# The order of a slot in a fused attention and mixture-of-experts kernel: first layer, second layer, then the attention's transposes, values and scores

## The chip, the cores and the metric

The kernel runs on one core of a Trainium2 chip. The metric is the time of one execution on the device in microseconds, the median of several runs. A core has the engines PE (matrix products, with its weight loads shown apart as PEld), DVE (vector), ACT (scalar functions), POOL (elementwise work of the GpSimd engine) and SP (here it only issues transfers). Each engine works its own instructions off in order and waits on semaphores for the others.

## What is computed

Sparse attention feeds a mixture of eight experts. Of the reference, cut:

```python
scores = scale * q @ k.T                       # 4 batches, 8 heads, 576 positions, 64 wide
scores = where(masks, scores, -1e9)            # heads 0-3: a local band of 32; heads 4-7: every 32nd position
attn = exp(scores - max); attn /= sum + 1e-9
x = (attn @ v) laid out as (2304, 512)
P = exp(x @ w_gate - max)                      # (2304, 8), then 8 rounds of row and column scaling
for e in range(8):
    out += P[:, e:e+1] * (relu(x @ w1[e]) @ w2[e])   # w1: 512 x 1024, w2: 1024 x 512
```

Products of the experts are made of three matmuls each, of operands split into a high and a low part (`split`: ACT writes the high part, POOL the difference).

## The kernel before

The attention is cut into 32 steps (`steps`, `NS`), each two heads by half a sequence. A step goes through these pieces: `at_scores` (PE, tile `sc`, line 251, in 64-row tiles of the array), `at_masks` (DVE, line 270, one instruction with its accumulator read per block), `at_exp` (ACT, line 281, one per block; a step has 4, 5 or 6 blocks), `at_normalize` (DVE lines 291 and 292, then a multiplication on POOL, line 293), `at_transpose` (PE, tile `tp`, line 303, then DVE copies to `pt`, lines 307 and 309), `at_values` (PE, tile `pv`, line 329, again in 64-row tiles), `x_high` (ACT, line 361) and `x_low` (DVE, line 366), which write the attention's output x into `reg`.

After a warm-up that runs the first eight steps, the rest of the attention is mixed with the first half of expert 0's hidden units in *slots*. Slot number s (0 to 35) does one 256-token chunk by one 128-wide piece `ft` of the hidden layer: `layer1` makes the product x·w1 (PE, tile `ph`, line 450, 12 matmuls) and `rectify` turns it into the hidden piece `h` (ACT, line 467: high part; DVE, line 468: low part); `layer2` multiplies the hidden piece of the slot before with w2 (PE, tile `y`, line 487, 6 matmuls; the last piece of a chunk is copied out by ACT, line 494 or 497, two copies). In slots 0 to 26 the attention rides along (`busy`): slot s takes the scores of step `at_k` = s + 8, the values of step `at_k - 3`, the transposes of step `at_k - 2` and the normalization of step `at_k - 1`. Where a chunk starts at a multiple of 512 tokens (slots 8, 16 and 24, `fresh`), its last block of x comes from the values of the same slot, so three quarters of the first layer (9 matmuls) stand at the slot's start and the last 3 behind the second layer.

The order in which the code of a slot is written is the order on every engine (`manual_schedule`): nothing is reordered later. Slots 0 to 3 also split the weights that are still missing (`late`: the last w1 piece in slot 0, the w2 pieces 1, 2, 3 in slots 1, 2, 3), at the slot's end, behind the step's exponentials on ACT and its multiplication on POOL; w2 piece `ft` is first read by the `layer2` of the next slot. In slots 5, 7, 9 to 12 and 18 to 23 a prepared sum of x blocks is split at the slot's end (`build_s`: ACT line 584, then DVE line 586). In slots 6, 13, 20 the gating's matmuls and in 7, 14, 21 its transposes are added (`next(gat)`).

PSUM is used in pairs of banks by tag: `l1` for `ph` and the gating, `y` and `s` for the second layer and the scores, `t` for the transposes and for the two value tiles of a step.

Of the kernel before, what the change touches and what calls it, by code (L numbers as in the profile page):

```python
# [8 lines left out]
F32 = mybir.dt.float32  # L9
# [57 lines left out]
def kernel(  # L67
# [10 lines left out]
    P = 128  # L78
# [14 lines left out]
    ps = ctx.enter_context(tc.tile_pool(name="ps", bufs=2, space=bass.MemoryType.PSUM))  # L93
# [62 lines left out]
    def store_x(n_parts):  # L156
        for _ in range(min(n_parts, len(done))):
            ci, k = done.pop(0)
            n = min(CH, NT - ci * CH)
            nc.sync.dma_start(  # L160
                xd[:, :, k, ci * CH : ci * CH + n], chunk(ci)[:, :, k].bitcast(F32)
            )
# [33 lines left out]
    def split_w(u, ft, which):  # L196
        src = raw.pop((u, ft, which))
        if which == 0:
            t = pools["w1"].tile([P, 2, NDT, P], F32R, tag="w1", name=f"w1_{u}_{ft}")
        else:  # L200
            t = w2t[:, 2 * D * ft : 2 * D * (ft + 1)].rearrange("p (b d) -> p b d", b=2)
        split(t[:, 0], t[:, 1], src)
        wt[u, ft, which] = t
# [9 lines left out]
    def load_qk(k):  # L213
        if k < NS:
            nq, nk, _ = _columns(*steps[k][1:])
            t = pools["qkv"].tile([P, QK], F32, tag="qk", name=f"qk_{k}", bufs=3)
            blocks = _blocks(*steps[k][1:])
            q0, ks, m = blocks[-1]
            end = nq + max(nk, ks[-1] + BR)
            nc.sync.dma_start(t[:, :end], qkv[k, :, :end])  # L220
            qk_t[k] = t
# [64 lines left out]
    def at_normalize(k):  # L286
        sm, n = sms[k]
        rs = sums_t.pop(k)[:, :n]
        if k in early:
            nc.vector.tensor_reduce(rs, sm[:, :n, :], axis=AX.X, op=ALU.add)  # L290
        nc.vector.tensor_scalar_add(rs, rs, 1e-9)
        nc.vector.reciprocal(rs, rs)
        nc.gpsimd.tensor_tensor(
            sm[:, :n, :], sm[:, :n, :], rs.unsqueeze(2).to_broadcast([P, n, BR]), op=ALU.mult
        )

    def at_transpose(k):
        sm, n = sms.pop(k)
        pt = pts[k] = pools["qkv"].tile([P, 3, P], F32, tag="pt", name=f"pt_{k}", bufs=3)
        tp = ps.tile([P, 3, P], F32, tag="t", name=f"tp_{k}")  # L300
        for c in range(0, n, 2):
            m = min(2, n - c)
            nc.tensor.transpose(  # L303
                tp[: m * BR, c // 2, :],
                sm[:, c : c + m, :].rearrange("p n k -> p (n k)"), ident,
            )
        nc.vector.tensor_copy(pt[:, : n // 2, :], tp[:, : n // 2, :])
        if n % 2:
            nc.vector.tensor_copy(pt[:BR, n // 2, :], tp[:BR, n // 2, :])
# [49 lines left out]
    def x_high(k):  # L359
        for src, (hi, _) in moved[k]:  # L360
            nc.scalar.activation(hi, src, AF.Copy)

    def x_low(k):
        b = steps[k][0]
        for src, (hi, lo) in moved.pop(k):
            nc.vector.tensor_tensor(lo, src, hi.bitcast(F32), op=ALU.subtract)
        p, hf = steps[k][1:]
        if hf:
            done.extend(
                (c, p) for c in range(NC) if b * S < min(NT, (c + 1) * CH) <= (b + 1) * S  # L370
            )
# [67 lines left out]
    def begin_layer1(u, c, ft, dts):  # L439
        c0, n = c  # L440
        k = u, c0, ft
        w = wt[u, ft, 0]
        first = k not in begun
        if first:
            begun[k] = ps.tile([P, 4 * P], F32, tag="l1", name=f"ph_{u}_{c0}_{ft}"), []
        ph, taken = begun[k]
        for dt in dts:
            taken.append(dt)
            for i, x in ((0, 0), (0, 1), (1, 0)):
                nc.tensor.matmul(  # L450
                    ph[:, :n], w[:, i, dt, :], xv(x, dt, c0, n),
                    start=(first and len(taken) == 1 and i + x == 0),
                    stop=(len(taken) == NDT and i == 1),
                )

    def layer1(u, c, ft, between=0):
        taken = begun[u, c[0], ft][1] if (u, c[0], ft) in begun else ()
        begin_layer1(u, c, ft, [dt for dt in range(NDT) if dt not in taken])
        for _ in range(between):
            next(gat)  # L460
        rectify(u, c, ft)

    def rectify(u, c, ft):
        c0, n = c
        ph = begun.pop((u, c0, ft))[0]
        h = pools["h"].tile([P, 2, 4 * P], F32R, tag="h", name=f"h_{u}_{c0}_{ft}")
        nc.scalar.activation(h[:, 0, :n], ph[:, :n], AF.Relu)
        nc.vector.scalar_tensor_tensor(
            h[:, 1, :n], ph[:, :n], 0.0, h[:, 0, :n].bitcast(F32), op0=ALU.max, op1=ALU.subtract
        )  # L470
        hs[u, c0, ft] = h
# [3 lines left out]
    def layer2(u, c, ft, only=None):  # L475
        c0, n = c
        nt = n // P
        if ft == 0 and (u, c0) not in ys:
            tags = ("y", "y", "s", "s")
            ys[u, c0] = [  # L480
                ps.tile([P, D], F32, tag=tags[i], name=f"y_{u}_{c0}_{i}") for i in range(nt)
            ]
        h, w = hs[u, c0, ft], wt[u, ft, 1]
        for i in range(nt) if only is None else only:
            y = ys[u, c0][i]
            for a, b, first in ((0, 0, True), (0, 1, False), (1, 0, False)):
                nc.tensor.matmul(  # L487
                    y, h[:, a, i * P : (i + 1) * P], w[:, b, :],
                    start=(ft == 0 and first), stop=(ft == FH - 1 and a == 1),
                )  # L490
            if ft == FH - 1:
                t = c0 // P + i
                if t < HEAD:
                    nc.scalar.activation(acc[:, t, :], y, AF.Copy)
                else:
                    o = acc[:, HEAD + t % STAGE, :]
                    nc.scalar.activation(o, y, AF.Copy)
                    outbox.append((yd[:, t - HEAD, :], o))
# [40 lines left out]
    for p in range(NPASS):  # L539
        for k in range(NK):  # L540
            k = (k - KEEP * p) % NK
# [527 lines left out]
    at_k = 0  # L1069

    def attention_scores():
        if at_k < NS:
            at_scores(at_k)
            at_masks(at_k)
            at_exp(at_k)

    def attention_rest():


        nonlocal at_k  # L1080
        if 0 <= at_k - 2 < NS:
            at_transpose(at_k - 2)
        if 0 <= at_k - 1 < NS:
            at_normalize(at_k - 1)
        at_k += 1

    def attention_values():
        if at_k > WARM + 2:
            store_x(1)
        if at_k > WARM + 1:  # L1090
            at_values(at_k - LAG, "tt")
            x_high(at_k - LAG)
            x_low(at_k - LAG)
        load_qk(at_k + 2)
        load_v(at_k)
# [66 lines left out]
    at_k = WARM + 1  # L1162
# [51 lines left out]
    slots = [(0, (c, 2 * P), ft) for c in range(0, NT, 2 * P) for ft in range(FH)]  # L1214
    prev, keep = None, []
    for slot, (u, c, ft) in enumerate(slots):
        busy = at_k < NS + LAG
        fresh = busy and ft == 0 and c[0] and c[0] % CH == 0
        if fresh:
            begin_layer1(u, c, ft, (0, 1, 2))  # L1220
        else:
            layer1(u, c, ft, ahead_of_second.get(slot, 0))
        if slot == 1:
            layer2(*prev, (0,))
        if busy:
            attention_values()
            attention_scores()
        if slot == 1:
            layer2(*prev, (1,))
        if slot == len(slots) - 1:  # L1230
            rest = [(prev, None), ((u, c, ft), None)]
        elif slot > 1:
            layer2(*prev)
        if fresh:
            begin_layer1(u, c, ft, (3,))
        if slot in (6, 7, 13, 14, 20, 21):
            next(gat)
        if slot < 2:
            load_w()
        if busy:  # L1240
            attention_rest()
            if fresh:
                rectify(u, c, ft)
            if slot in late:
                split_w(*plain[late[slot]])
            if slot == 5:
                split_gate()
            if at_k == NS + LAG:
                store_x(len(done))
                open_pools("right", ("hg", 8))  # L1250
        for x in work.get(slot, ()):
            x()
        send, keep = keep, []
        for x in send:
            nc.sync.dma_start(*x)
        keep, outbox[:] = outbox[:], []
        prev = (u, c, ft)
# [136 lines left out]
```

## Time and profile before

| | us |
|---|---|
| median of 3 runs (1534.41 to 1534.9) | 1534.9 |
| the profiled execution's own time | 1533.58 |
| its span on the engines | 1531.8 |
| PE busy | 1522.9 |
| DVE busy | 1302.4 |
| POOL busy | 1042.1 |
| ACT busy | 546.2 |

Shares of the whole span say little about the slots, which are its first tenth; the stretch is read by its own rows. In a row of the order of time, the first number is the start and the second how long the merged group lasted; matmuls overlap, so what a group of them costs PE is the distance from its first start to the start of the next group. What stands in brackets is the idle time of that engine just before, and what ended it.

### The profile page before, as it was taken

To read this page: it belongs to the slowest core of one execution; us is meant where nothing else is said; L and a number is where in the kernel's file an instruction comes from. 1 tells how busy PE (TensorE), PEld (TensorE's weight loads), DVE (VectorE), ACT (ScalarE), POOL (GpSimd) and SP (SyncE) were. 2 spreads that over 40 slices of the span, in tenths; PEclk is the share of its full clock that TensorE was granted. 3 is DMA by queue.
4 is the path that set the end of the run, shared out by engine and by line. 5 is a ranking of instruction groups with operands and counts; after the bars stand their busy time and mean duration, and the time that the engine had idled before them with its cause. 6 is when DMAs were issued, how large, how long until landed. Compare 5 with 4: busy or idle time off the path is not lost.

```text
span 1531.8 us, 27904 instructions
## 1 busy us (share of the span) xinstructions
PE 1522.9 (99%) x10099; PEld 1446.4 (94%) x10099; DVE 1302.4 (85%) x2611; ACT 546.2 (36%) x1340; POOL 1042.1 (68%) x1055
## 2 busy tenths in 40 slices
PE   8999999999999999999999999999999999999999
PEld 6888989898999999999999999999999999999998
DVE  6665899999999999768888888888688888888888
ACT  7675344343443434242332222322323232222221
POOL 4566155656556565078888888888687787777874
PEclk9999999999999999999999999999999999999999
DMA  9878888888898888886877867777576676666662
GB/s 279 254 236 274 313 315 315 338 315 337 309 337 316 321 318 314 320 312 259 313 259 283 308 239 292 298 255 277 211 306 262 261 286 240 264 266 238 276 247 90
DMA packets 145625, 431.11 MB, mean 281 GB/s; under 512 B 35696, under 2 KB 89168, under 8 KB 130512
## 3 DMA queue, kind: packets, MB, share of 16 engines
q1 hardware_dynamic: 145200, 429.14, 75.3%
q8 instruction: 80, 1.31, 0.3%
q14 instruction: 57, 0.47, 0.1%
q10 hardware_dynamic: 288, 0.20, 0.0%
HBM read 284.54 MB, written 144.75 MB: 280 GB/s over the span
## 4 chain that ended last, share of the span: by engine, by line
PE 98%; DVE 1%; ACT 0%; DMA 0%; issue 0%; POOL 0%; SPq 0%; ACTq 0%; POOLq 0%; DVEq 0%
PE p L882 27%; PE bb L731 18%; PE yg L763 18%; PE bc L731 12%; PE ba L731 12%; PE y L487 3%; PE ph L450 3%; PE pv L329 1%; PE sc L251 1%; PE pl L378 1%; PE tp L303 1%; PE tr L912 0%; PE unread L1119 0%; DMA qk<-in_qkv 0%; ACT sm L281 0%
## 5 line engine op out<-in xcount | busy, mean ns | idle before, releaser
L890 DVE TENSOR_TENSOR total<-p,total 128x384 f32<-128x384 f32 x770 | 401.0, 557 | 0.8 <-PE p L882 0.8
L731 PE MATMUL bb<-reg 128*128 128x384 f32 x1620 | 326.3, 336 | 0.0
L731 PEld LDWEIGHTS bb<-reg 128*128 128x128 f32 x1620 | 285.2, 188 | 2.9 <-DVE u L805 0.3
L731 PE MATMUL bc<-reg 128*128 128x384 f32 x1080 | 216.3, 334 | 0.0
L731 PE MATMUL ba<-reg 128*128 128x384 f32 x1080 | 216.2, 334 | 0.0
L863 ACT ACTIVATE a<-u 128x384 fp32r<-128x384 f32 x114 | 59.9, 526 | 384.5 <-DVE u L857 382.7
L805 DVE TENSOR_TENSOR u<-bb,m 128x384 f32<-128x384 f32 x180 | 99.8, 554 | 110.9 <-PE bb L731 109.5
L731 PEld LDWEIGHTS bc<-reg 128*128 128x128 f32 x1080 | 190.1, 188 | 0.0
L731 PEld LDWEIGHTS ba<-reg 128*128 128x128 f32 x1080 | 190.0, 188 | 0.0
L939 POOL TENSOR_TENSOR s1t<-m,u 128x384 f32<-128x384 f32 x57 | 57.9, 1016 | 163.3 <-DVE m L857 163.3
L770 DVE SCALAR_TENSOR_TENSOR acc<-yg,gate,acc 128x512 f32<-128x512 f32 x197 | 139.1, 740 | 9.0 <-PE yg L763 9.0
L763 PE MATMUL yg<-w2t,h 128*128 128x512 f32 x540 | 125.5, 390 | 0.0
L763 PE MATMUL yg<-w2b,h 128*128 128x512 f32 x540 | 125.4, 390 | 0.0
L882 PE MATMUL p<-s,w2b 128*128 128x384 f32 x696 | 125.3, 334 | 0.0
L882 PEld LDWEIGHTS p<-s,w2b 128*128 128x128 f32 x696 | 121.1, 188 | 0.0
L882 PE MATMUL p<-s,w2t 128*128 128x384 f32 x672 | 121.0, 334 | 0.0
L763 PEld LDWEIGHTS yg<-w2t,h 128*128 128x128 f32 x540 | 101.1, 188 | 20.5
L763 PEld LDWEIGHTS yg<-w2b,h 128*128 128x128 f32 x540 | 101.1, 188 | 20.5
L867 POOL TENSOR_TENSOR a<-u,a 128x384 fp32r<-128x384 f32 x114 | 117.0, 1026 | 0.0
L882 PEld LDWEIGHTS p<-s,w2t 128*128 128x128 f32 x672 | 116.9, 188 | 0.0
L194 POOL TENSOR_TENSOR reg<-ra,reg 128x512 fp32r<-128x512 f32 x28 | 48.1, 1719 | 89.3 <-ACT reg L193 89.3
L805 DVE TENSOR_TENSOR u<-bc,u 128x384 f32<-128x384 f32 x180 | 99.4, 552 | 4.5 <-PE bc L731 1.4
(154 smaller groups left out, 2810.2 us busy)
## 6 DMA issues: line engine op xcount, KB each, us to landing
reg<-wd SPq DMA_DIRECT2D x56, 1792.0 KB
wd<-reg SPq DMA_DIRECT2D x30, 1792.0 KB
w2b<-w2d SPq DMA_DIRECT2D x27, 1792.0 KB
w2t<-w2d SPq DMA_DIRECT2D x26, 1792.0 KB
w2d<-w2b SPq DMA_DIRECT2D x15, 2048.0 KB
w2d<-w2t SPq DMA_DIRECT2D x15, 2048.0 KB
raws<-in_w SPq DMA_DIRECT2D x68, 256.0 KB
reg<-sd SPq DMA_DIRECT2D x12, 768.0 KB
```

Of the source, the lines that this page charges most:

```text
L194: nc.gpsimd.tensor_tensor(lo, src, hi.bitcast(F32), op=ALU.subtract)
L450: nc.tensor.matmul(ph[:, :n], w[:, i, dt, :], xv(x, dt, c0, n), start=(first and len(taken) == 1 and i + x == 0), stop=(len(taken) == NDT ...
L487: nc.tensor.matmul(y, h[:, a, i * P : (i + 1) * P], w[:, b, :], start=(ft == 0 and first), stop=(ft == FH - 1 and a == 1),)
L731: nc.tensor.matmul(out[:, :TN], w[:, i, k, :], xops[x][:, xi, k, :], start=(start and n == 0), stop=(n == 5), skip_group_check=True,)
L763: nc.tensor.matmul(y, hg[g, i // 3, f][:, a, o : o + P], w[:, b, f, :], start=(f == 0 and a + b == 0), stop=(f == 1 and a == 1),)
L770: nc.vector.scalar_tensor_tensor(acc[:, i, :], y, gate[:, t, e : e + 1], acc[:, i, :], op0=ALU.mult, op1=ALU.add)
L805: nc.vector.tensor_tensor(o, bank[:, :TN], s, op=ALU.add)
L863: nc.scalar.activation(t[:, 0], src, AF.Copy)
L867: nc.gpsimd.tensor_tensor(t[:, 1], src, t[:, 0].bitcast(F32), op=ALU.subtract)
L882: nc.tensor.matmul(y[:, :TN], w[:, b, wi, d, :], h[:, a, :], start=(a + b == 0), stop=(a == 1),)
L890: nc.vector.tensor_tensor(o, y[:, :TN], o, op=ALU.add)
L939: nc.gpsimd.tensor_tensor(s1, m1, u3, op=ALU.add)
```

## The change

In a slot, the second layer moves ahead of the attention. Behind it the attention's transposes and the normalization come first, then values and scores; they were the slot's end before. In a fresh slot the transposes also move to the front of the attention, and the second layer stays behind it. Slots 0 and 1 keep their order. From slot 2 on, the transposes' tile is taken from the pair of banks `l1` in place of `t`.

```diff
--- before.py
+++ after.py
@@ -294,10 +294,10 @@
             sm[:, :n, :], sm[:, :n, :], rs.unsqueeze(2).to_broadcast([P, n, BR]), op=ALU.mult
         )
 
-    def at_transpose(k):
+    def at_transpose(k, tag="t"):
         sm, n = sms.pop(k)
         pt = pts[k] = pools["qkv"].tile([P, 3, P], F32, tag="pt", name=f"pt_{k}", bufs=3)
-        tp = ps.tile([P, 3, P], F32, tag="t", name=f"tp_{k}")
+        tp = ps.tile([P, 3, P], F32, tag=tag, name=f"tp_{k}")
         for c in range(0, n, 2):
             m = min(2, n - c)
             nc.tensor.transpose(
@@ -1074,15 +1074,11 @@
             at_masks(at_k)
             at_exp(at_k)
 
-    def attention_rest():
-
-
-        nonlocal at_k
+    def attention_turn(tag="t"):
         if 0 <= at_k - 2 < NS:
-            at_transpose(at_k - 2)
+            at_transpose(at_k - 2, tag)
         if 0 <= at_k - 1 < NS:
             at_normalize(at_k - 1)
-        at_k += 1
 
     def attention_values():
         if at_k > WARM + 2:
@@ -1220,17 +1216,23 @@
             begin_layer1(u, c, ft, (0, 1, 2))
         else:
             layer1(u, c, ft, ahead_of_second.get(slot, 0))
+        if slot == len(slots) - 1:
+            rest = [(prev, None), ((u, c, ft), None)]
+        elif slot > 1 and not fresh:
+            layer2(*prev)
         if slot == 1:
             layer2(*prev, (0,))
         if busy:
+            if slot > 1:
+                attention_turn("l1")
             attention_values()
             attention_scores()
-        if slot == 1:
-            layer2(*prev, (1,))
-        if slot == len(slots) - 1:
-            rest = [(prev, None), ((u, c, ft), None)]
-        elif slot > 1:
-            layer2(*prev)
+            if fresh:
+                layer2(*prev)
+            if slot == 1:
+                layer2(*prev, (1,))
+            if slot < 2:
+                attention_turn()
         if fresh:
             begin_layer1(u, c, ft, (3,))
         if slot in (6, 7, 13, 14, 20, 21):
@@ -1238,7 +1240,7 @@
         if slot < 2:
             load_w()
         if busy:
-            attention_rest()
+            at_k += 1
             if fresh:
                 rectify(u, c, ft)
             if slot in late:
```

The first of three places is PE in slots 2 and 3. `ph_0_0_2` is slot 2's first layer, `y_0_0_0` and `y_0_0_1` are the two token tiles of the second layer, `tp_8` the transposes of step 8, `pv_7` the values of step 7, `sc_10` the scores of step 10. Before:

```order
L450 MATMUL ph_0_0_2_796<-reg_107,w1_0_2_582 128x256 x12
L329 MATMUL pv_7_0_813<-pt_7_784,v_7_585 64x32 x2
...
L251 MATMUL sc_10_0_846<-qk_10_658 64x64 x2
...
L487 MATMUL y_0_0_0_713<-w2t_106,h_0_0_1_710 128x512 x3
L487 MATMUL y_0_0_1_714<-w2t_106,h_0_0_1_710 128x512 x3
L303 MATMUL tp_8_882<-cst_97,sm_8_682 128x128 x2
L450 MATMUL ph_0_0_3_891<-reg_107,w1_0_3_704 128x256 x12
```

With the change:

```order
L450 MATMUL ph_0_0_2_796<-reg_107,w1_0_2_582 128x256 x12
L487 MATMUL y_0_0_0_713<-w2t_106,h_0_0_1_710 128x512 x3
L487 MATMUL y_0_0_1_714<-w2t_106,h_0_0_1_710 128x512 x3
L303 MATMUL tp_8_819<-cst_97,sm_8_682 128x128 x2
L329 MATMUL pv_7_0_827<-pt_7_783,v_7_585 64x32 x2
...
L251 MATMUL sc_10_0_860<-qk_10_658 64x64 x2
...
L450 MATMUL ph_0_0_3_891<-reg_107,w1_0_3_704 128x256 x12
```

The second layer, and with it the first reader of the w2 piece split in the slot before, follows the first layer at once; values and scores stand behind it.

The second place is DVE in slots 9 and 10, from the low part of slot 9's sum (`so`) to the masks of step 18. `pt_15` and `pt_16` are copies of transposes, `sums_16` and `sums_17` row sums for the normalization, `reg_107<-pv_15` is x's low part. Before:

```order
L307 COPY pt_15_1571<-tp_15_1572 128x256
L309 COPY pt_15_1571<-tp_15_1572 64x128
L291 TENSOR_SCALAR sums_16_1442<-sums_16_1442 128x4
L292 RECIPROCAL sums_16_1442<-sums_16_1442 128x4
L586 TENSOR_TENSOR so_0_0_128_1581<-sx_0_0_128_1479,so_0_0_128_1581 128x512
L468 SCALAR_TENSOR_TENSOR h_0_512_2_1604<-ph_0_512_2_1591,h_0_512_2_1604 128x256
L366 TENSOR_TENSOR reg_107<-pv_15_0_1608,reg_107 128x192
L366 TENSOR_TENSOR reg_107<-pv_15_1_1609,reg_107 128x128
L270 ISA sm_18_1654,mx_18_1655<-sc_18_0_1639,cst_97 128x64
```

With the change:

```order
L586 TENSOR_TENSOR so_0_0_128_1581<-sx_0_0_128_1479,so_0_0_128_1581 128x512
L468 SCALAR_TENSOR_TENSOR h_0_512_2_1604<-ph_0_512_2_1591,h_0_512_2_1604 128x256
L307 COPY pt_16_1613<-tp_16_1614 128x256
L291 TENSOR_SCALAR sums_17_1570<-sums_17_1570 128x4
L292 RECIPROCAL sums_17_1570<-sums_17_1570 128x4
L366 TENSOR_TENSOR reg_107<-pv_15_0_1622,reg_107 128x192
L366 TENSOR_TENSOR reg_107<-pv_15_1_1623,reg_107 128x128
L270 ISA sm_18_1668,mx_18_1669<-sc_18_0_1653,cst_97 128x64
```

The copies and the two operations on the row sums stood between the masks and the sum's low part; now they stand between the hidden piece's low part and x's.

The third place is PE in the fresh slot 8. Before:

```order
L450 MATMUL ph_0_512_0_1389<-reg_107,w1_0_0_417 128x256 x9
L329 MATMUL pv_13_0_1399<-pt_13_1376,v_13_1114 64x54 x2
...
L487 MATMUL y_0_256_1_1143<-w2t_106,h_0_256_3_1298 128x512 x3
L450 MATMUL ph_0_512_0_1389<-reg_107,w1_0_0_417 128x256 x3
L303 MATMUL tp_14_1465<-cst_97,sm_14_1239 128x128 x2
L303 MATMUL tp_14_1465<-cst_97,sm_14_1239 64x128
L450 MATMUL ph_0_512_1_1486<-reg_107,w1_0_1_499 128x256 x12
L329 MATMUL pv_14_0_1503<-pt_14_1464,v_14_1213 64x32 x2
```

With the change:

```order
L450 MATMUL ph_0_512_0_1389<-reg_107,w1_0_0_417 128x256 x9
L303 MATMUL tp_14_1400<-cst_97,sm_14_1254 128x128 x2
L303 MATMUL tp_14_1400<-cst_97,sm_14_1254 64x128
L329 MATMUL pv_13_0_1409<-pt_13_1307,v_13_1132 64x54 x2
...
L487 MATMUL y_0_256_1_1090<-w2t_106,h_0_256_3_1298 128x512 x3
L450 MATMUL ph_0_512_0_1389<-reg_107,w1_0_0_417 128x256 x3
L450 MATMUL ph_0_512_1_1486<-reg_107,w1_0_1_499 128x256 x12
L487 MATMUL y_0_512_0_1502<-w2t_106,h_0_512_0_1474 128x512 x3
```

The last three matmuls of slot 8's first layer still wait for x from the values of this slot, whose low part DVE now writes behind the copies and the normalization; slot 9's second layer, which reads slot 8's hidden piece, follows slot 9's first layer at once.

## Rows read from the trace of the kernel before

**Rows 1.** The page: its span, and the chain that ended last, by engine.

```profile
span 1531.8 us, 27904 instructions
...
PE 98%; DVE 1%; ACT 0%; DMA 0%; issue 0%; POOL 0%; SPq 0%; ACTq 0%; POOLq 0%; DVEq 0%
```

**Rows 2.** Busy time by stretch: PE, PEld, DVE, ACT, POOL, granted clock, DMA share, GB/s.

```profile
10.00:20.00 10.00, 7.78 (x262) 6.43 (x251) 8.74 (x69) 8.85 (x44) 5.39 (x7) 1.00 0.91 279
```

**Rows 3.** PE in order of time, slots 9 to 11 (start, length, group).

```profile
63.51 1.67 PE L450 MATMUL ph<-reg,w 128*128 128x256 f32 x12
65.11 0.89 PE L329 MATMUL pv<-pt,v 64*64 64x32 f32 x40
...
66.31 1.66 PE L487 MATMUL y<-w2t,h 128*128 128x512 f32 x6
67.81 0.49 PE L303 MATMUL tp<-cst,sm 128*128 128x128 f32 x3
68.05 1.67 PE L450 MATMUL ph<-reg,w 128*128 128x256 f32 x12
...
72.47 0.72 PE L450 MATMUL ph<-reg,w 128*128 128x256 f32 x4
```

**Rows 4.** PE in order of time, a slot without attention.

```profile
155.26 1.68 PE L450 MATMUL ph<-reg,w 128*128 128x256 f32 x12
156.77 1.55 PE L487 MATMUL y<-w2t,h 128*128 128x512 f32 x6
```

**Rows 5.** All engines in order of time, slots 2 to 5.

```profile
32.59 2.07 PE L487 MATMUL y<-w2t,h 128*128 128x512 f32 x6
...
33.23 0.99 PEld L487 LDWEIGHTS y<-w2t,h 128*128 128x128 f32 x5 [0.46 <-POOL w2t L194]
...
34.63 1.68 PE L450 MATMUL ph<-reg,w 128*128 128x256 f32 x12
...
36.23 0.67 PE L329 MATMUL pv<-pt,v 64*64 64x32 f32 x32
...
37.21 1.92 PE L487 MATMUL y<-w2t,h 128*128 128x512 f32 x6
...
37.69 0.99 PEld L487 LDWEIGHTS y<-w2t,h 128*128 128x128 f32 x5 [0.29 <-POOL w2t L194]
...
39.10 1.67 PE L450 MATMUL ph<-reg,w 128*128 128x256 f32 x12
...
40.28 0.83 POOL L293 TENSOR_TENSOR sm<-sm,sums 128x384 f32<-128x384 f32 x1 [2.64 <-DVE sums L292]
...
42.40 1.01 PEld L487 LDWEIGHTS y<-w2t,h 128*128 128x128 f32 x5 [0.54 <-POOL w2t L194]
...
43.92 0.84 PE L450 MATMUL ph<-reg,w 128*128 128x256 f32 x5
```

**Rows 6.** DVE and ACT in order of time, from the masks of slot 9 to those of slot 10.

```profile
66.88 0.21 DVE L270 CUSTOM_DVE_ANT_0 sm<-sc,cst 128x64 f32<-128x64 f32 x1
...
67.14 0.35 ACT L281 ACTIVATE sm<-sm,mx 128x64 f32<-128x64 f32 x1 [0.60 <-DVE mx L270]
...
68.33 0.42 DVE L307 COPY pt<-tp 128x256 f32<-128x256 f32 x1 [0.79 <-PE tp L303]
...
68.94 0.63 ACT L584 ACTIVATE so<-sx 128x512 fp32r<-128x512 f32 x1 [0.36 <-POOL sx L581]
...
69.60 0.97 DVE L586 TENSOR_TENSOR so<-sx,so 128x512 fp32r<-128x512 f32 x1 [0.36 <-ACT so L584]
...
70.49 0.41 DVE L468 SCALAR_TENSOR_TENSOR h<-ph,h 128x256 fp32r<-128x256 f32 x1
...
70.95 0.55 DVE L366 TENSOR_TENSOR reg<-pv,reg 128x192 fp32r<-128x192 f32 x2
...
71.42 0.21 DVE L270 CUSTOM_DVE_ANT_0 sm<-sc,cst 128x64 f32<-128x64 f32 x1
```

**Rows 7.** ACT in order of time, slot 8: the two copies of a finished chunk.

```profile
63.67 1.06 ACT L494 ACTIVATE acc<-y 128x512 f32<-128x512 f32 x2
```

## The prediction

> **What bounds the kernel now.** I read the page first: PE carries 98% of the chain that ended last [rows 1], so anything that makes PE wait is paid in full, and what falls on another engine costs only where PE comes to wait for it. The time by stretch tells that the granted clock was 1.00 even where PE was busy for 7.78 us of 10 [rows 2]. Then the slots, in order of time on PE: in slot 9 the distances from group to group are 1.60 us for the first layer, 1.20 for values and scores, 1.50 for the second layer, 0.24 for the transposes, 4.54 in all [rows 3]; nothing is left between the groups that looks like a wait. The exceptions are slots 2, 3 and 4: there the second matmul of the second layer waits for POOL's low part of the w2 piece (L194 on w2t), and starts at 33.23, 37.69 and 42.40 [rows 5]. Last, DVE and ACT in a slot with a sum to split [rows 6], because the change reorders them too.
>
> The profiled execution took 1533.58 us by its own time, with a span of 1531.8; the median of the runs is 1534.9, 1.3 above it. I make the sum against 1533.6 and add 1.3. The measurement of this kernel can tell about 0.2%, 3.1 us, from no change.
>
> **What the change removes and adds.** No instruction, byte or transfer is added or dropped; 24 slots are reordered, and the loads and stores that SP issues keep their order among themselves. Four parts count.
>
> *The edges between full-array and 64-row matmuls.* Before, a slot goes from first layer to values and from scores to second layer; now from transposes to values and from scores to first layer: one entry and one exit either way. An entry costs 0.09: a first layer ahead of values takes 1.60 [rows 3], ahead of a second layer 1.51 [rows 4]. I take 0 for the difference, and 0.09 per slot either way as bounds, 24 x 0.09 = 2.2 us.
>
> *Slots 2 to 4, the w2 piece.* The split of a w2 piece stands behind the exponentials of the slot before, on ACT and then POOL, and its reader now comes ahead of values and scores, which so far ran while PE had to wait anyway. In slot 2 the wait ends as before at 33.23, since nothing ahead of it moved. Before, slot 3 began 1.40 later (34.63). Now values and scores, 1.20 by [rows 3], follow, with 0.15 for the entry (the 0.09 and a little for the transposes' last columns): slot 3 begins at 36.0, 1.4 late. From there it is a ring: scores, masks, exponentials, split on ACT, split on POOL, second layer, values, scores. Before, the reader's second matmul started 5.10 after the end of the scores in slot 3 (32.59 to 37.69) and 5.19 in slot 4 (37.21 to 42.40) [rows 5]. So slot 3's starts at 36.0 + 5.1 = 41.1, and slot 4 begins 1.41 + 0.98 + 0.15 later (old distance to the next first layer; values and scores, 36.23 to 37.21; entry), at 43.6 instead of 39.10. In slot 4 POOL's multiplication, 0.83 long, ran just ahead of the split's low part [rows 5]; it is now issued earlier, so I take 5.2 - 0.8: second matmul at 48.0, slot 5 at 48.0 + 1.52 + 0.98 + 0.15 = 50.7 instead of 43.92. That is **6.8 us**; 7.6 without POOL's 0.8, and 5.5 if each ring is another 0.6 shorter.
>
> *The fresh slots 8, 16, 24.* The last 3 matmuls of the first layer need x's low part, and DVE now writes it behind the copies of the transposes and the normalization, which in turn stand behind the sum's low part of the slot before. Pieces from [rows 3, 6]: masks begin 0.57 after the scores' end (66.31 to 66.88), the first exponential 0.26 later, 0.36 per block (four of them end at 68.94 - 0.36 = 68.58), the sum's high part 0.63, a hand-over of 0.03, its low part 0.89 until DVE goes on, copies and normalization 0.91 (68.33 to 69.60 - 0.36), x's low part 0.47. For slot 8, five blocks: 0.57 + 0.26 + 1.80 + 0.63 + 0.03 + 0.89 + 0.91 + 0.47 = 5.6 after slot 7's scores. PE is there after 9 of 12 matmuls (1.2), transposes 0.24, values and scores 1.20, second layer 1.50: 4.1. Wait 1.4. Next, the hidden piece of slot 8: masks at 5.6, then 0.26, four exponentials 1.44, the two copies of a finished chunk 1.06 [rows 7], about 0.4 for the ReLU: 8.7; its reader, slot 9's second layer, was 1.2 us of values and scores later and now comes at 5.6 + 0.4 + 1.6 = 7.6. Wait 1.1. Slot 16 follows a slot without a sum, so 1.55 falls away: no first wait, the second is 7.2 - 6.1 = 1.0. Slot 24 has no scores of its own: PE is there after 3.7, the first wait is 1.9, and the second goes. Together **5.4 us**; bounds 2 (half of it hidden, since these chains sum worst cases) and 8.
>
> *The slots with a sum to split, 5, 7, 9 to 12, 18 to 23.* Here DVE and ACT form a ring of one slot: masks, exponentials, sum high, sum low, hidden piece low, x low, next masks. Before, without the 0.36 that ACT waited for POOL, it is 0.26 + 1.44 + 0.63 + 0.03 + 0.89 + 0.46 + 0.47 = 4.2 with four blocks and 4.5 with five [rows 6], about PE's slot of 4.54: covered. The copies and the normalization lay beside the exponentials; now they lie in the ring, 0.91 more: 5.4. A slot of PE gains a lag of 0.9 on each. PE starts to pay when the hidden piece's low part comes later than the next first layer that needs its bank: it ended at 70.90 [rows 6] and that began at 72.47 [rows 3], so 1.57 is cover. Slots 9 to 12: 4 x 0.9 - 1.57 = 2.0. Of 18 to 23, two hold the gating's matmuls and are longer on PE; four count, another 2.0. Slots 5 and 7 stand alone and are covered. Together **4.0 us**; bounds 0 (the lag stays covered) and 7. In slots without a sum the ring is 4.4 with five blocks: covered. Taking `tp` from the first pair of banks costs nothing that I find: the bank it takes was last read by a slot's hidden piece or by the copies of the transposes, a slot earlier; what it was to give, fewer waits of the values for the `t` pair, the steady slots do not show as a wait.
>
> Sum: 0 + 6.8 + 5.4 + 4.0 = 16.2; 1533.6 + 16.2 + 1.3 = **1551 us**.
>
> **Rivals.** *First, the ring of w2 alone.* If DVE and ACT keep enough lead, the last two parts vanish: 1533.6 + 6.8 + 1.3 = 1541.7. For it speaks that steady slots show no wait now; against it the ring of 5.4 against 4.54. *Second, the edges decide, and it is not slower.* If grouping transposes, values and scores let both edges go, that would give back 0.09 at the entry and I allow as much at the exit: 24 x 0.18 = 4.3, and with the last two parts covered 6.8 - 4.3 leaves +2.5, 1537.4, within what cannot be told. It would decide from 0.16 per slot on; the number of edges speaks against it. *Third, the clock.* PE now waits for about 3 us in slots 3 and 4. If the granted clock fell to 1.2 GHz there and a slot of 4.5 us ran at that level after each, up to 2 x 4.5 = 9 more: 1560. Against it: the clock stayed at 1.00 with 2.2 us of 10 not busy [rows 2]. The Trainium skill, page "TensorE: Matmul & The Clock Gate", section "Part 1: The HAM clock gate (the "warmup" mystery)", states that a half-rate clock is the default and activity releases it, which speaks for this rival: by that rule, if these waits count as idle, the time would be the 1560; the trace shows no fall so far. That the change does not do what it says can be left out: the order of the instructions shows it.
>
> **How the numbers follow.** Forecast 0.78, first rival 0.10, second 0.04, third 0.05, and 0.03 for what I don't see, 0.02 of it faster and 0.01 no change. The low bounds of the parts give 5.5 + 2 + 0 - 2.2 = 5.3 (1540), the high ones 7.6 + 8 + 7 + 2.2 = 25 (1560); that all lie at one end is unlikely, so 1545 to 1557 is the forecast's own range, and 1541 to 1558 takes in the first rival and leaves the third out. Slower by over 0.2%: 0.78 + 0.10 + 0.05 = 0.93; within: 0.05; faster: 0.02.
>
> **What would show it.** In the profile after: the distance from slot 2's first layer to slot 5's grows by about 7 us, with PE or its weight loads waiting for POOL's L194 on w2t, about three times 1 to 3 us; behind each fresh slot's first layer waits for DVE's x (L366), and then of the second layer for ACT's or DVE's hidden piece (L467, L468); in slots 10 to 13 and 19 to 22 some tenths each before the first layer. Past slot 27 nothing changes but the start. I am wrong if slots 2 to 4 together grow by under 4 us, if slots 9 to 13 show no wait, or if the slots without waits differ from 4.54 and 4.42 by more than 0.1.

## The result, and the profile after

The changed kernel takes 1549.51 us (median of 5 runs, 1549.28 to 1551.84) against 1534.9 (5 runs, 1533.98 to 1535.49): 14.6 us more, a ratio of 1.0099 with a 95% interval of 1.0085 to 1.0113. The profiled execution took 1549.28 with a span of 1547.5. The page of the changed kernel, span and the chain that ended last by engine, answers to [rows 1]:

```profile
span 1547.5 us, 27910 instructions
...
PE 94%; ACT 3%; DVE 2%; issue 0%; POOL 0%; DMA 0%; ACTq 0%
```

PE had 98% of that chain; 4% of 1547 us, some 60 us, now run through ACT and DVE in its place. A chain runs through them for the whole time that they take, not only for the part that PE waits. What PE lost is read from the slots: the distance from the start of a slot's first layer (L450 on ph) to the start of the next one's, after less before. Of slot 0's first layer the warm-up makes the first nine matmuls; its start is that of the last three. This table has the distances in us for groups of slots, for the changed kernel and for the twelve of the experiments (E1 to E12); "others" are the rest of slots 0 to 26. From slot 28 on no distance in slots differs by more than 0.02.

| kernel | median us (runs) | ratio to before | 2 to 4 | 8, 9 | 16, 17 | 24, 25 | 6, 13, 20 | 7, 14, 21 | others | sum |
|---|---|---|---|---|---|---|---|---|---|---|
| the change | 1549.5 (5) | 1.0099 | 7.59 | 2.05 | 1.54 | 1.85 | 1.72 | -0.73 | 1.35 | 15.36 |
| E1 pair t | 1573.8 (5) | 1.0259 | 9.62 | 4.51 | 1.89 | 4.52 | 4.83 | 1.48 | 10.56 | 37.40 |
| E2 old in 2 to 4 | 1543.1 (5) | 1.0054 | 0.00 | 2.05 | 1.56 | 1.86 | 1.91 | -0.74 | 1.36 | 8.00 |
| E3 only transposes | 1539.8 (5) | 1.0038 | 0.13 | 1.42 | 0.91 | 1.71 | 1.19 | -0.14 | 0.12 | 5.35 |
| E4 early splits | 1542.5 (5) | 1.0051 | 0.02 | 2.05 | 1.54 | 1.86 | 1.70 | -0.72 | 1.40 | 7.85 |
| E5 sum ahead | 1542.5 (5) | 1.0060 | 7.30 | 0.58 | 1.61 | 0.29 | 0.36 | -0.72 | -0.13 | 9.29 |
| E6 old in 8, 9, ... | 1545.9 (5) | 1.0081 | 7.79 | 0.33 | 0.62 | 1.40 | 1.88 | -0.74 | 1.85 | 13.13 |
| E7 before, early splits | 1532.7 (11) | 0.9993 | -1.19 | 0.03 | -0.02 | 0.00 | 0.01 | 0.01 | -0.01 | -1.17 |
| E8 = E4 + E5 | 1535.5 (11) | 1.0012 | 0.00 | 0.58 | 1.64 | 0.29 | 0.36 | -0.72 | -0.13 | 2.02 |
| E9 = E8, w1 elsewhere | 1536.1 (1) | | 0.02 | 0.58 | 0.74 | 0.28 | 0.36 | -0.72 | 0.47 | 1.73 |
| E10 = E8, h first | 1535.2 (1) | | 0.02 | 0.14 | 1.17 | 0.29 | 0.36 | -0.73 | -0.15 | 1.10 |
| E11 = E8, copies late | 1537.6 (1) | | 0.03 | 1.42 | 2.47 | 0.29 | 0.36 | -0.72 | -0.14 | 3.70 |
| E12 one early split | 1546.1 (1) | | 5.23 | 2.05 | 1.53 | 1.86 | 1.73 | -0.74 | 1.35 | 13.00 |

Where two kernels do the same thing, their entries agree to some hundredths (2.05 in four of them), which the medians cannot offer: those are comparable to about 0.2%. The sum leaves out the warm-up ahead of slot 0, which no edit touches, and what stands behind the slots. Slot 0 started between 0.36 us earlier (E1) and 2.29 later (E2) than before, 0.65 later in the changed kernel, whose granted clock was 0.91 over the first 20 us; from slot 28 to the end the executions differ from the one before by -0.80 (E8) to 0.25 (E9).

Slots 2 to 5 on PE in order of time in the changed kernel, against [rows 5]:

```profile
30.45 1.68 PE L450 MATMUL ph<-reg,w 128*128 128x256 f32 x12
32.53 0.50 PE L487 MATMUL y<-w2t,h 128*128 128x512 f32 x1 [0.41 <-ACT w2t L193]
33.88 1.43 PE L487 MATMUL y<-w2t,h 128*128 128x512 f32 x5 [0.85 <-POOL w2t L194]
...
36.65 1.68 PE L450 MATMUL ph<-reg,w 128*128 128x256 f32 x12
40.22 0.50 PE L487 MATMUL y<-w2t,h 128*128 128x512 f32 x1 [1.89 <-ACT w2t L193]
41.57 1.71 PE L487 MATMUL y<-w2t,h 128*128 128x512 f32 x5 [0.85 <-POOL w2t L194]
...
45.34 1.95 PE L450 MATMUL ph<-reg,w 128*128 128x256 f32 x12
48.16 0.50 PE L487 MATMUL y<-w2t,h 128*128 128x512 f32 x1 [0.87 <-ACT w2t L193]
49.51 1.42 PE L487 MATMUL y<-w2t,h 128*128 128x512 f32 x5 [0.85 <-POOL w2t L194]
...
52.16 1.70 PE L450 MATMUL ph<-reg,w 128*128 128x256 f32 x12
```

The second layer now waits for both parts of its w2 piece, high (ACT) and low (POOL), in each of the three slots. From the second wait's end to the next first layer it takes 2.77 in slot 2 (33.88 to 36.65), 2.65 in slot 4 (49.51 to 52.16), and 3.77 in slot 3 (41.57 to 45.34). The stretches of the changed kernel tell why (columns as in [rows 2], the granted clock third from the end):

```profile
36.00:42.00 6.00, 3.27 (x56) 2.64 (x50) 2.15 (x18) 3.45 (x17) 1.88 (x2) 1.00 0.52 174
42.00:46.00 4.00, 4.00 (x62) 3.16 (x61) 1.62 (x12) 0.62 (x3) 0.83 (x1) 0.57 0.02 4
46.00:48.00 2.00, 1.29 (x11) 1.09 (x10) 0.37 (x6) 2.00 (x11) 0.00 (x0) 1.00 0.58 175
```

PE was busy for 3.27 of 6 us; behind that the granted clock fell to the 1.2 GHz level for most of 42 to 46, and was back by 46. It cost about 1.06 us, 3.77 less 2.71, the mean of its neighbours.

The other waits of PE in the changed kernel, as totals from 53 us to 170 us (what waits, for what, us in total, times, longest):

```profile
PE y L487 <- ACT h L467: 2.0, 2, 1.0
PE ph L450 <- DVE reg L366: 1.6, 2, 1.2
PE pl L378 <- DVE h L468: 1.0, 2, 0.7
PE ph L450 <- DVE h L468: 1.0, 2, 0.6
PE tp L303 <- POOL sm L293: 0.4, 1, 0.4
```

The first two are those of the fresh slots (L366 writes x's low part, L467 the hidden piece). The next two are gating products and first layers whose bank the hidden piece's low part (L468) still reads. The last stands in slot 24, where the transposes wait for the multiplication of their own step on POOL. Slots without waits are as long as before: slots 10 and 22 differ by 0.01, slot 5 by nothing.

### The profile page after: what moved, and what is told of

The parts are those of the page before. It is cut to its first block, busy times and chain, and to the rows that moved or that the text cites. A ratio compares the mean times of both kernels' runs of the same rounds, so it can differ in the third digit from the quotient of the medians.

```text
span 1547.5 us, 27910 instructions
## 1 busy us (share of the span) xinstructions
PE 1527.4 (99%) x10099; PEld 1447.6 (94%) x10099; DVE 1298.6 (84%) x2611; ACT 544.3 (35%) x1340; POOL 1040.1 (67%) x1055
## 4 chain that ended last, share of the span: by engine, by line
PE 94%; ACT 3%; DVE 2%; issue 0%; POOL 0%; DMA 0%; ACTq 0%
PE p L882 27%; PE bb L731 18%; PE yg L763 17%; PE bc L731 12%; PE ba L731 12%; PE y L487 2%; PE ph L450 2%; ACT sm L281 2%; PE pv L329 1%; DVE reg L366 1%; PE pl L378 1%; DVE so L586 0%; PE sc L251 0%; PE tr L912 0%; ACT so L584 0%
```

## The experiments

Each edit is made on the changed kernel unless said otherwise; the ratios' intervals reach 0.0014 to either side at most.

**E1, the transposes' tile stays in pair t.**

```diff
             if slot > 1:
-                attention_turn("l1")
+                attention_turn()
```

> The change's order in every slot, but the transposes' tile stays in the pair of banks t, as before the change. Theory on record (the pair of banks neither costs nor gives anything): 1549.5, within 3 us. Rival: the tile of the transposes holds one of t's two banks until DVE has copied it out, and the values, which now follow at once, need both. In the trace of the changed kernel the copies end 0.7 us after the values' start in slot 5 (55.50 to 56.22) and 0.95 in slot 10 (81.83 to 82.78); such a wait in each of 25 slots is 17 to 24 us, so 1567 to 1574, with PE or its weight loads waiting for L307 or L309 ahead of L329 in every slot.

1573.8 us, ratio 1.0259 (1.0245 to 1.0273), as the rival said. The two largest of the waits of PE from 20 us to 180 us, and slot 8 in order of time:

```profile
PE pv L329 <- issue: 11.1, 12, 2.4
PE pv L329 <- DVE pt L307: 10.4, 14, 1.5
...
```

```profile
73.41 0.32 PE L329 MATMUL pv<-pt,v 64*64 64x54 f32 x4
...
75.11 0.42 DVE L307 COPY pt<-tp 128x256 f32<-128x256 f32 x1
75.45 0.27 DVE L309 COPY pt<-tp 64x128 f32<-64x128 f32 x1
...
75.82 0.69 PE L329 MATMUL pv<-pt,v 64*64 64x54 f32 x16 [2.09 <-issue]
```

Four matmuls of the values run, then the second value tile waits until L309 has emptied the bank of the transposes; all 12 waits that the profile puts down to "issue" end 0.10 us after such an L309, the 14 others 0.06 at most after L307. These 26 waits are 21.5 us; the first two, 0.9 us, are the warm-up's and stand in the kernel before too. The table's sums differ by 22.0. Some of that is the clock, which was at 0.50 from 42 us to 48 us and again from 76 us to 79 us. So the line on the bank, which costs nothing, gives some 20 us in this order.

**E2, slots 2 to 4 in the old order.**

```diff
-        elif slot > 1 and not fresh:
+        elif slot > 4 and not fresh:
...
-            if slot > 1:
+            if slot > 4:
                 attention_turn("l1")
...
-            if fresh:
+            if fresh or 1 < slot < 5:
                 layer2(*prev)
...
-            if slot < 2:
+            if slot < 5:
                 attention_turn()
```

> Slots 2, 3 and 4 go back to the order before the change; the change starts at slot 5. Theory on record (the ring of the w2 pieces is priced by itself): what the first layers' starts show as lost in slots 2 to 4, 7.6 us (21.71 against 14.12 from slot 2's first layer to slot 5's), goes, about 1 us of which is the granted clock that fell in slot 3: 1542, within 1.5, and slots 5 to 26 still lose 7.8. Rival: the late start gave DVE and ACT slack that the later slots live on, or the other way round; then slots 5 to 26 lose another sum, 11 for 1545 or more, 5 for 1539 or less. The granted clock should be 1.00 in slots 2 to 4.

1543.1, ratio 1.0054 (1.0042 to 1.0067). All of the 7.59 goes, the clock is at 1.00 from 30 us to 55 us, and the later groups are unchanged but for 0.2 in slot 6. So the parts are independent. (In the warm-up of this execution 0.75 was granted from 10 us to 20 us, and slot 0 came late by 2.29.)

**E3, only the transposes and the normalization move.**

```diff
-        elif slot > 1 and not fresh:
-            layer2(*prev)
...
-            if fresh:
-                layer2(*prev)
...
+        if 1 < slot < len(slots) - 1:
+            layer2(*prev)
         if fresh:
             begin_layer1(u, c, ft, (3,))
```

> Only the transposes and the normalization move ahead of the values (pair l1); the second layer stays behind the scores in every slot from 2 on. Theory on record: the w2 pieces are read behind values and scores again, so the 7.6 us of slots 2 to 4 go; the second layer behind the scores gives 1.5 us more cover to the slots with a sum, so their 2.3 go; the first waits of the fresh slots (for x's low part) stay with the copies ahead of it, the second ones (for the hidden piece) go, since its reader comes 1.4 us later: 2.6 stay, 1537.5. Rival: the hidden piece of a fresh slot is late for whoever needs it; the transposes of the next slot take the bank that it leaves, and wait in place of the second layer, so the fresh slots keep most of their 5.4: 1541. The row that decides: the wait ahead of slot 9's L303, for L468 or L467.

1539.8, ratio 1.0038 (1.0025 to 1.0051), between the two and nearer the rival. All but 0.13 of the 7.59 goes, and of slots 11, 12 and 19, which lose 0.44, 0.20 and 0.71 in the changed kernel, nothing stays; but the fresh groups keep 4.04 of 5.44, and the wait has changed hands (PE, slots 8 and 9):

```profile
63.61 1.94 PE L450 MATMUL ph<-reg,w 128*128 128x256 f32 x15
66.67 0.52 PE L303 MATMUL tp<-cst,sm 128*128 128x128 f32 x3 [1.12 <-DVE h L468]
```

The fresh slot's hidden piece is late; the second layer, now behind values and scores, no longer waits for it, but the transposes do. They read nothing of it, so what they wait for is the bank that it frees.

**E4, the w2 pieces split early.**

```diff
             attention_values()
+            if slot in late and slot > 0:
+                split_w(*plain[late[slot]])
             attention_scores()
...
-            if slot in late:
+            if slot == 0:
                 split_w(*plain[late[slot]])
```

> The change's order; the splits of the w2 pieces (slots 1, 2, 3) are issued behind the values, ahead of the step's scores, masks and exponentials, in place of the slot's end. Theory on record (the readers wait because the split stands behind the exponentials on ACT and then POOL): the high part is written some 2 us earlier, so the second layers of slots 2 to 4 find it; 5.5 to 7.6 of the 7.6 us of these slots go: 1543, within 1.5. Rival: what bounds slots 2 to 4 is the arrival of the w2 pieces or the second layer's own place ahead of the attention, and an earlier split doesn't help: 1549; or the exponentials, now later by 0.6, lose it again in the slots behind: 1546.

1542.5, ratio 1.0051 (1.0038 to 1.0063): 0.02 in place of 7.59, the order unchanged, nothing lost behind. Slot 2's second layer runs without a wait, and slot 3's keeps a short one (PE):

```profile
32.25 1.66 PE L487 MATMUL y<-w2t,h 128*128 128x512 f32 x6
...
37.48 1.44 PE L487 MATMUL y<-w2t,h 128*128 128x512 f32 x5 [0.30 <-POOL w2t L194]
```

The place of the split behind the exponentials is the cause.

**E5, the sums split ahead of the exponentials.** The generator `build_s` gets a stop between L584 and L586, and `front` names the slots, each one later than before:

```diff
+            for w in front.get(slot, ()):
+                next(w)
             attention_scores()
+            for w in front.get(slot, ()):
+                next(w)
```

> The change's order; only the split of a prepared sum is issued elsewhere: one slot later, its high part (ACT, L584) ahead of the step's exponentials and its low part (DVE, L586) behind the masks, so that it is no longer a link between the exponentials and the hidden piece. Theory on record (DVE and ACT form a ring of one slot, with the sum's two parts in it): without them the ring is some 1.2 us shorter than PE's slot allows for, so the 2.3 us outside slots 2 to 4 and the fresh ones go, and the fresh slots 8 and 24, whose chains have the sum's parts in them, give back 1 to 2 us each; slots 16 and 17, which follow a slot without a sum, keep their 1.5. In all 5 to 6 less: 1544, within 1.5. Rival: the copies of the transposes between the hidden piece and x's low part do it alone, whatever stands behind the exponentials: then slots 12 and 20 keep their 0.4 and 0.7 and the time is 1548 or more.

1542.5, ratio 1.0060 (1.0048 to 1.0073). What PE still waits for between 53 us and 175 us:

```profile
PE y L487 <- ACT h L467: 1.2, 2, 1.0
PE tp L303 <- POOL sm L293: 0.4, 1, 0.4
```

6.07 goes: all of "others", 1.36 of the gating slots, 1.47 of slots 8 and 9, 1.56 of 24 and 25; slots 16 and 17, whose chain has no sum in it, stay. Each of these groups came as expected.

**E6, the old order in the fresh slots and the slot behind each.** With `old = (8, 9, 16, 17, 24, 25)`:

```diff
-        elif slot > 1 and not fresh:
+        elif slot > 1 and slot not in old:
...
-            if slot > 1:
+            if slot > 1 and slot not in old:
                 attention_turn("l1")
...
-            if fresh:
+            if slot in old:
                 layer2(*prev)
...
         if busy:
+            if slot in old:
+                attention_turn()
             at_k += 1
```

> The change's order, but the fresh slots 8, 16, 24 and the slot behind each (9, 17, 25) have the order before the change, transposes at the end and in pair t. Theory on record: the 5.4 us of these six slots go and the rest (7.6 in slots 2 to 4, 2.3 elsewhere) stays: 1544, within 1. Rival: going to the old order and back costs waits of its own at the borders (the values of slot 10 and 18 behind copies that are just made, the lag of DVE that slot 7's sum leaves): 2 or more of the 5.4 stay, 1546 or more.

1545.9, ratio 1.0081 (1.0067 to 1.0094): 2.35 of 5.44 stay, and slot 18 loses 0.46 where it lost 0.02, as the rival said. Slot 24 still waits, now for x's high part on ACT (PE):

```profile
149.71 0.39 PE L450 MATMUL ph<-reg,w 128*128 128x256 f32 x1 [0.71 <-ACT reg L361]
```

ACT comes to it at 149.23, right behind the high part of the sum of the slot ahead (L584, from 148.71): the lag that ACT brings from there is paid whatever the order inside.

**E7, the kernel before with the edit of E4.**

> The kernel before with one edit: the splits of the w2 pieces are issued ahead of the step's scores and exponentials, as in the earlier run with early splits. Theory: the weight loads of slots 2 to 4 waited 0.46, 0.29 and 0.54 for POOL's low part, 1.3 us in all, of which the pipelining of PE's loads hides some; 0.5 to 1.3 less, 1534 against 1534.9, which the times can't tell; the distance from slot 2's first layer to slot 5's tells it, 13.0 to 13.6 in place of 14.12. Rival: the exponentials, 0.6 us later, delay the hidden piece or the copies and the distance stays or grows.

1532.7 (11 runs, 1531.92 to 1535.9) against 1534.06 (21 runs): ratio 0.9993 (0.9985 to 1.0002), which the times can't tell, but slots 2 to 4 are 1.19 shorter. The second layer's six matmuls are one group in each slot, with no wait (PE):

```profile
33.30 1.65 PE L487 MATMUL y<-w2t,h 128*128 128x512 f32 x6
...
37.50 1.65 PE L487 MATMUL y<-w2t,h 128*128 128x512 f32 x6
...
41.71 1.65 PE L487 MATMUL y<-w2t,h 128*128 128x512 f32 x6
```

**E8, E4 and E5 together.**

> The change's order with both edits: the w2 pieces split early and the sums split ahead of the exponentials. Theory on record (the order itself costs nothing; what costs is the work of ACT, DVE and POOL that it no longer covers): 1549.5 less 7.5 (slots 2 to 4) less 5 to 6: 1536.5, within 1.5, near the kernel before. Rival: one lag hides behind the other, and once the first is gone the second shows in full, so the sum of the two gains isn't reached: 1539 or more.

1535.5 (11 runs), ratio 1.0012 (1.0003 to 1.0020): the gains add, 15.36 becomes 2.02. Most of what the order cost was the place of the splits. It is not free, though: E7 gives the order before the same early w2 splits, and against it E8 is 3.2 us longer in the slots (2.02 and 1.17). The edit of E5 was not run on the order before. The 1.64 left in slots 16 and 17 are the object of E9 to E11, one execution each, read by the table. ACT there, in E8:

```profile
100.09 0.61 ACT L193 ACTIVATE reg<-raws 128x512 fp32r<-128x512 f32 x1
...
100.61 0.52 ACT L361 ACTIVATE reg<-pv 128x96 fp32r<-128x96 f32 x4
...
103.09 1.05 ACT L497 ACTIVATE acc<-y 128x512 f32<-128x512 f32 x2
104.05 0.37 ACT L467 ACTIVATE h<-ph 128x256 fp32r<-128x256 f32 x1
```

**E9, the w1 pieces of slots 14 to 17 split elsewhere, on E8.** The pieces of slots 15 and 16 move to 13 and 18.

```diff
-    for g, i, pieces_at in ((0, 5, (14, 15, 16, 17)), (1, 22, (24, 25, 26, 27))):
+    for g, i, pieces_at in ((0, 5, (13, 14, 17, 18)), (1, 22, (24, 25, 26, 27))):
```

> The kernel with sums and w2 pieces split early, and one more edit: the four pieces of the next w1 group that are split at the ends of slots 14 to 17 (L193 on reg, 0.61 on ACT behind the exponentials) move to slots 13, 14, 17 and 18. With sums and w2 pieces early, slots 16 and 17 still lose 1.64, and there x's high part (L361) starts 0.52 us behind the start of such a piece, right at its end (100.09 and 100.61). Theory: ACT's work behind the exponentials is what makes x late, here as with the sums; without the piece the first wait, 0.45, goes and the second, 1.19, loses 0.3 to 0.5: 0.7 to 0.9 stay. Theory on record (x's low part waits behind DVE's copies and normalization): the two slots keep their 1.6. One look; the distance from slot 16's first layer to slot 18's decides.

0.74 in place of 1.64. x's high part now follows the exponentials at once (ACT):

```profile
99.33 0.33 ACT L281 ACTIVATE sm<-sm,mx 128x64 f32<-128x64 f32 x1
...
99.67 0.52 ACT L361 ACTIVATE reg<-pv 128x96 fp32r<-128x96 f32 x4
```

The piece put into slot 18 makes slot 19 0.60 longer instead, about its 0.61 on ACT: a control that came unasked.

**E10, the hidden piece ahead of the finished chunk's copies, on E8.** `layer2` holds the two copies back in a fresh slot:

```diff
             if fresh:
                 rectify(u, c, ft)
+                copy_out()
```

> The kernel with sums and w2 pieces split early, and one more edit: in the fresh slots ACT writes the hidden piece's high part ahead of the two copies of the finished chunk, in place of behind them. Theory: the 1.05 us of these copies (103.09 to the hidden piece at 104.05) are a link of the chain to slot 17's second layer; with them behind, that waits for the first copy's bank instead of the hidden piece, about 0.5 earlier: slots 16 and 17 lose 1.1 in place of 1.64, slots 8 and 9 nothing in place of 0.58 less the 0.2 of the first wait. Rival: the low part of the hidden piece or the banks of the second layer come last anyway: no change. One look.

1.17 in slots 16 and 17 and 0.14 in 8 and 9, as expected. With a sum of 1.10 this is the least that the new order lost.

**E11, copies and normalization behind x's low part in the fresh slots, on E8.**

```diff
             attention_values()
+            if fresh:
+                attention_turned()
             attention_scores()
```

> The kernel with sums and w2 pieces split early, and one more edit: in the fresh slots DVE's copies of the transposes and the normalization are issued behind x's low part, in place of ahead of it. Theory on record (x's low part is late because these stand ahead of it): the first waits of the three fresh slots, 0.22, 0.45 and 0.39, go, about 1.0 us in all. Rival, from the rows of the earlier run, where x's high part ended after DVE was done with both: x is late because ACT is, nothing goes, and the masks, now behind the copies, come 0.5 to 0.9 later and lengthen the second waits: 1 to 2.5 us more. One look; the distances from each fresh slot's first layer to the second slot behind decide.

The sum is 1.68 more than E8's, as the rival said. In slot 16, ACT's high part (L361) still ends last, DVE having long been idle, and the copies now hold up the masks (ACT and DVE in order of time; the added lines shift these numbers by 8):

```profile
101.13 0.52 ACT L369 ACTIVATE reg<-pv 128x96 fp32r<-128x96 f32 x4
...
101.48 0.61 DVE L374 TENSOR_TENSOR reg<-pv,reg 128x96 fp32r<-128x96 f32 x4 [2.00 <-ACT reg L369]
...
102.01 0.41 DVE L315 COPY pt<-tp 128x256 f32<-128x256 f32 x1
```

**E12, only slot 3's w2 piece split early.**

```diff
             attention_values()
+            if slot == 2:
+                split_w(*plain[late[slot]])
             attention_scores()
...
-            if slot in late:
+            if slot in (0, 1, 3):
                 split_w(*plain[late[slot]])
```

> The change's order; only the piece that slot 3 reads is split early (the one of slot 2), the pieces that slots 2 and 4 read are split at the slots' ends. Theory on the clock: the granted clock fell in slot 3 because PE stood still there the longest (1.89 and 0.85 us, PE busy for 3.27 us of 36 to 42); without that wait it stays at 1.00, and slots 2 to 4 lose 1.37 in slot 2, some 0.3 in slot 3 and in slot 4 a wait like the one of the changed kernel, 2.0 to 2.4: 3.6 to 4.1 in place of 7.59. Rival: a fall comes behind slot 4's wait then, with 1 us more in slots 4 and 5. One look.

5.23 in slots 2 to 4, as the rival said. Slot 3 loses 0.32, and the clock falls one slot later (PE, then the stretches):

```profile
43.67 0.49 PE L487 MATMUL y<-w2t,h 128*128 128x512 f32 x1 [1.34 <-ACT w2t L193]
45.02 2.50 PE L487 MATMUL y<-w2t,h 128*128 128x512 f32 x5 [0.85 <-POOL w2t L194]
...
48.99 1.69 PE L450 MATMUL ph<-reg,w 128*128 128x256 f32 x12
```

```profile
42.00:45.00 3.00, 0.82 (x4) 0.31 (x3) 0.42 (x1) 1.89 (x10) 1.27 (x1) 0.91 0.71 248
45.00:48.00 3.00, 2.98 (x8) 2.15 (x8) 0.00 (x0) 1.04 (x2) 0.00 (x0) 0.52 0.25 96
```

The five matmuls took 2.50 where they take 1.42 or 1.43 at full clock.

## Why the prediction was right

The predicted 1551 is 1.5 above the measured 1549.5, and the cause is the one named: no added work, but PE standing still for ACT, DVE and POOL. The parts are not as near as their sum. The clock, which the sum left out, took 1.06; the slots with a sum cost 0.9 less than forecast, and 0.73 came back in slots 7, 14 and 21. That these largely cancel is luck. Term by term:

- **The edges, 0 predicted.** Right: slots without waits are unchanged. Slots 7, 14 and 21 even gain 0.24 each, which was not in the sum; the gating's transposes follow the scores there now. In E3, where the second layer stands between the two, 0.05 at most is left of it; why the pairing is cheaper no run shows.
- **Slots 2 to 4, 6.8 predicted, 7.59 measured.** The ring was right in mechanism (E2 and E4 each remove it) and nearly in size: less the clock's 1.06 it is 6.5. The second matmul of slot 3 was forecast at 41.1 and came at 41.57, 0.18 early if the 0.65 by which slot 0 started later is taken off.
- **The fresh slots, 5.4 predicted, 5.44 measured.** The three pairs were forecast at 2.5, 1.0 and 1.9 and lost 2.05, 1.54 and 1.85, so that two misses of about 0.5 cancel. In slot 24 the wait for x was 1.23, and 0.39 is the transposes' wait for POOL, which was not in the working. The chain through the sum's parts is shown (E5 takes 3.0 of it). Slot 16's first wait was not foreseen: there a w1 piece on ACT delays x (E9), which the working did not list. That the copies and the normalization alone make x late is not borne out: with the sums out of the way, E11 gains nothing by moving them. With the sums in place that was not tried; in slot 8 of the changed kernel both stand in the chain:

```profile
69.91 0.61 ACT L584 ACTIVATE so<-sx 128x512 fp32r<-128x512 f32 x1
...
70.43 0.52 ACT L361 ACTIVATE reg<-pv 128x112 fp32r<-128x112 f32 x4
70.56 0.69 DVE L586 TENSOR_TENSOR so<-sx,so 128x512 fp32r<-128x512 f32 x1 [1.64 <-ACT so L584]
71.17 0.42 DVE L307 COPY pt<-tp 128x256 f32<-128x256 f32 x1
...
71.99 0.59 DVE L366 TENSOR_TENSOR reg<-pv,reg 128x112 fp32r<-128x112 f32 x4
...
72.55 1.93 PE L450 MATMUL ph<-reg,w 128*128 128x256 f32 x14 [0.39 <-DVE reg L366]
```

- **The slots with a sum, 4.0 predicted, about 3.1 measured.** The ring is there (E5 removes it) but shorter than forecast: from one L586 to the next, with DVE at work or waiting for ACT all the time, 4.60 with five exponentials and 5.10 with six, against 5.4 with five. In the ring of 4.60, L586 held DVE for 0.70 in place of 0.89, the hidden piece's low part for 0.33 in place of 0.46, copies and normalization for 0.63 in place of 0.91 (no second copy, L309, in most of these slots), x's low part for 0.37 in place of 0.47, and from the masks to the next L586 it took 2.57 in place of 2.72: 0.85 in all. The working took its pieces from one slot: L586 lasted 0.97 there, but 0.69 in six of its twelve executions in the kernel before. The ring is paid in other places too: 1.35 in slots 11, 12 and 19, nothing in 10, 1.72 in the gating slots 6, 13 and 20, whose product needs a bank of the same pair. DVE in slots 10 to 12 and the wait on PE, in the changed kernel:

```profile
81.41 0.69 DVE L586 TENSOR_TENSOR so<-sx,so 128x512 fp32r<-128x512 f32 x1 [1.59 <-ACT so L584]
...
86.51 0.77 DVE L586 TENSOR_TENSOR so<-sx,so 128x512 fp32r<-128x512 f32 x1 [1.97 <-ACT so L584]
...
87.67 1.70 PE L450 MATMUL ph<-reg,w 128*128 128x256 f32 x12 [0.36 <-DVE h L468]
...
91.11 0.69 DVE L586 TENSOR_TENSOR so<-sx,so 128x512 fp32r<-128x512 f32 x1 [1.78 <-ACT so L584]
```

- **The bank, nothing predicted.** Right for this change, since it costs nothing; but the text stopped at what the pair l1 costs and did not ask what the new order would cost without it. E1 says some 20 us.
- **The third rival, the clock.** Its mechanism came, but once in the slots, for 1.06 us instead of 9. The Trainium skill, page "TensorE: Matmul & The Clock Gate", section "Part 1: The HAM clock gate (the "warmup" mystery)", was cited there for a half-rate default that activity releases; the trace agrees, with 0.57 granted in 42 to 46 us behind a stretch in which PE was busy for 3.27 of 6 us.

## What to carry to other kernels

When work on the bounding engine is reordered, price what the other engines' chains then lack in cover, not the moved instructions: here 13 of 15 us came from splits queued behind exponentials, for two edits that moved only those splits gave them back. A tile moved to another pair of banks is part of the order, so ask what the order costs without it. And such an edit may help the old order too: E7, the kernel before with early splits, is 1.2 us shorter in slots 2 to 4, though its times alone can't tell it from no change.

## What the runs showed of the hardware that was not expected

The granted clock can fall to the 1.2 GHz level inside a busy program, behind waits of PE of one to two microseconds. In the changed kernel it fell behind slot 3's waits (1.89 and 0.85 us), not behind those of slot 2 (0.41 and 0.85) or slot 4 (0.87 and 0.85). In E12 it fell before the second of slot 4's waits (1.34 and 0.85) was over: 0.91 was granted from 42 to 45 us, and PE went on at 45.02. With the waits gone or short (E2, E4, E8) the stretches between 30 and 48 us show 1.00. All four profiled executions with the changed order in slots 2 to 4 have the fall (0.91 from 30 to 48 us in the changed kernel, E5 and E6, 0.83 in E1).

One fall took about 3 us at the lower level; in E1 the level was low throughout 42 to 48 us. A fall cost 1.1 us in the changed kernel and, by the same distance, 1.3 in E12 (3.97, from 45.02 to 48.99, in place of 2.65).

The same code does not always bring a fall, though. The warm-up is the same in all of these kernels, and from 10 to 20 us 0.83 was granted in the changed kernel, E4 and E8 and 0.75 in E2, but 1.00 in the kernel before, E5 and E7. What decides it these runs leave open.
